# Output products of the first pair of blocks: 512 tokens streamed past 128 weight columns, and three attention steps moved

## The chip, the core and the metric

The kernel runs on one core of a Trainium2 chip. The metric is the device time of one execution in microseconds. Engines: TensorE (PE; its weight loads are listed as PEld), VectorE (DVE), ScalarE (ACT), GpSimd (POOL) and SyncE (SP), which only issues DMAs.

## What is computed

Attention over 4 batches, 8 heads of width 64, 512 local and 32 global tokens, then two dense layers over the 4 x 544 = 2176 rows of width 512:

```python
mask = np.abs(pos[:, None] - pos[None, :]) <= 32          # local queries: a window of 32, and all global keys
x = attention(q, k, v).reshape(2176, 512)                  # global queries see all keys
h = x @ moe_w_in                                           # 512 -> 2048
x = (np.maximum(h, 0) + alpha * np.minimum(h, 0)) @ moe_w_out
h = x @ moe2_w_in                                          # 512 -> 2048
out = (h * np.clip(h + 3.0, 0.0, 6.0) / 6.0) @ moe2_w_out
```

Everything is float32. The kernel splits every operand of the dense layers into a high part of reduced width (fp32r) and the low rest, and sums three products (high x high, high x low, low x high) in place of one.

## The kernel before

**Blocks.** The tokens come in five blocks: block 0, 1 and 2 are the 512 local tokens of batches 0, 1 and 2; block 3 is the first half of batch 3, block 4 its second half with the 128 global rows. Layer one runs block by block (the loop at the end of fused_kernel). In each step s an inner tile of 12 matmuls (h_tile, L590), its activation on ScalarE and VectorE (act, L600 to L609), and two steps later (LAG) an output group of 12 matmuls (y_tiles, L621) are issued. During block 0 the weights of layer one, which arrive as 64-bit numbers, are converted on ScalarE and VectorE (begin_float32, end_float32, L114 to L137); the same is done for layer two's weights during blocks 1 to 4 (second_weights), with the sums that Strassen's scheme wants; the results go to DRAM (wi, wo).

**Attention in between.** attention_steps(n), L639, runs n steps of the generator local_units; STEPS says how many there are in each step of a block. The units (batch, half, head pair) are taken in 16 pairs. For pairs 4 to 15 STARTS gives the step in which the scores are computed and WAITS how many steps later the value products follow: pair 5 has STARTS 4 and WAITS 4, pair 13 has STARTS 33 and WAITS 5. Step 1 of that list runs in step s = 4 of block 0, so step 8 is s = 11 there, step 32 is the last step with an inner tile of block 1 (s = 15), and step 33 the first of block 2. For pairs from 5 on the probabilities are turned: the step after the scores, VectorE transposes 32x32 blocks (turned, L285) and POOL sends the tile to DRAM (turn_out, L185); a step later POOL fetches it back in four pieces (turn_in, L191). The results of these pairs' value products (values, L299; the division L311; the block transpose L324) go the same way, except pair 7's, whose results, like pair 4's, are left as they are (L319) and turned by TensorE:

```python
steps[at][0].append((scores, *pairs[j]))
steps[at + wait][0].append((values, *pairs[j]))
```

**The change of blocks.** At s = end - 1 the loop makes sure that attention has come far enough (ready), calls x_transposed (L535), which issues TensorE's transposes of the results that are still unturned (L550, into a bank xt_ps), and then this step's y_tiles. At the last step x_split (L554) makes the next block's operands on ScalarE (L562) and VectorE (L563). All scores, value products, inner tiles and xt_ps take their turn in four PSUM banks (bank, tag "ps"); the outputs y have the other four.

**Layer two** (second_layer) works on two pairs of blocks in turn, twos: the first pair is blocks 1 and 2 (n = 0, 1024 tokens), the second block 0 with blocks 3 and 4 (n = 1, end is true). Each pair is a Strassen product of seven products with 512-token halves. First the inner products (product, L947): a weight part of 128 columns is loaded, 512 tokens stream past it. Then the output sums (summed, L1025): for each of the seven products and four groups k of inner rows, the operand is split into hi and lo (parts_of, L957: ScalarE L960, VectorE L961, three buffers), and for jp in 0 and 1 and each chunk c of 128 tokens three matmuls are issued:

```python
mm = nc.tensor.matmul(bank, lhsT=part[:, jp, 128 * c:128 * c + 128],
                      rhs=wo[:, jp, 256 * wl:256 * wl + 256], start=opens, ...
```

So 128 tokens are the loaded weight and 256 weight columns stream; the result has tokens on the partitions and is stored as it is (store, L1058: four DMAs of 128 rows and 256 columns per result, four results per pair). ScalarE copies or VectorE adds the sums out of PSUM (each, L1048; add, L877). Between the groups of the first pair, further work on the second pair's operands is issued (MORE, inputs, L774 to L793). In the second pair the 128 global rows ("the rest") have products of their own beside it (rest_in, L899; rest_out, L920). take (L854) keeps up to six weight tiles (512 KB each, ws) loading ahead through SyncE's queue, the one that the stores use too.

**Order.** Each engine works through its own queue in order. The program is written in the order above, and a planner then orders each engine's queue by its own estimate of times; instructions under here(...) keep their program order among themselves.

Of the kernel before, what the change touches and what calls it, by code (L numbers as in the profile page):

```python
# [19 lines left out]
S = SL + SG  # L20
# [16 lines left out]
STARTS = [0, 4, 8, 12, 16, 19, 22, 25, 29, 33, 36, 39]  # L37
GLOBAL = [[(x[0], int(x[1])) for x in part.split()] for part in "s0|t0|i0 s1|o0 t1|i1 s2|t2|o1 i2 s3|t3|o2 i3||o3".split("|")]
WAITS = [4, 4, 5, 4, 5, 5, 5, 5, 5, 5, 5, 5]
# [21 lines left out]
def fused_kernel(ctx, tc, qkE, vE, qgz, kN, vN, vgN, w1, w2, consts, out):  # L61
# [805 lines left out]
    def second_layer(bt):  # L867
# [45 lines left out]

        def rest_out(y, i, k, wo):

            kind, half = REST_OF[i]
            for jp in range(2):
                j = 2 * (2 * k + jp) + kind
                for wl, gl in ((0, 0), (1, 0), (0, 1)):
                    mm = nc.tensor.matmul(y[:, 256 * half:256 * half + 256],  # L920
                                     lhsT=gr[j // 4][:, gl, 128 * (j % 4):128 * (j % 4) + 128],
                                     rhs=wo[:, jp, 256 * wl:256 * wl + 256], start=i == k == jp == wl == gl == 0,
                                     stop=i in (2, 7) and k == NP // 2 - 1 and jp == gl == 1, skip_group_check=True)
                    if i == len(PRODUCTS) and k == jp == wl == gl == 0:
                        here(mm)
# [10 lines left out]
        for n, two in enumerate(twos):  # L936
# [43 lines left out]

            coming, split = operands(), []
# [43 lines left out]
            def summed(i, y, first=True):  # L1025
                for k in range(NP // 2):
# [3 lines left out]
                    for jp in range(2):  # L1030
                        for c in range(chunks):
                            bank = y[c // 2][:, 256 * (c % 2):256 * (c % 2) + 256]
                            for wl, part in ((0, hi), (1, hi), (0, lo)):
                                opens = first and k == jp == c % 2 == 0 and (wl, part is hi) == (0, True)
                                mm = nc.tensor.matmul(bank, lhsT=part[:, jp, 128 * c:128 * c + 128],  # L1035
                                                      rhs=wo[:, jp, 256 * wl:256 * wl + 256], start=opens,
                                                      stop=k == NP // 2 - 1 and jp == 1 and part is lo,
                                                      skip_group_check=True)
                                if opens and i == c == 0:
                                    here(mm)  # L1040
# [7 lines left out]
            def each(f, *lists):  # L1048
                for k, banks_ in enumerate(zip(*lists)):
                    f(slice(512 * k, min(512 * k + 512, 256 * chunks)), *banks_)  # L1050
# [4 lines left out]
            def cols(b, s_):  # L1055
                return b[:, 0:s_.stop - s_.start]

            def store(r, th, dm):  # L1058
                for c in range(chunks):
# [9 lines left out]
            each(lambda s_, b: nc.scalar.copy(m1[:, s_], cols(b, s_)), x_)  # L1069
            summed(1, y_)  # L1070
            m5 = result()
            each(lambda s_, b: nc.scalar.copy(m5[:, s_], cols(b, s_)), y_)
            summed(2, x_, False)
            c11 = result()
            each(lambda s_, b: nc.scalar.copy(c11[:, s_], cols(b, s_)), x_)
# [5 lines left out]
            each(lambda s_, b: add(m1[:, s_], m1[:, s_], cols(b, s_)), z_)  # L1081
            summed(4, y_, False)
            c12 = result()
            each(lambda s_, b: add(c12[:, s_], m1[:, s_], cols(b, s_)), y_)
# [4 lines left out]
            each(lambda s_, b: add(u3_[:, s_], m1[:, s_], cols(b, s_)), w_)  # L1089
# [5 lines left out]
            each(lambda s_, b: add(m1[:, s_], m1[:, s_], cols(b, s_)), w_)  # L1095
# [24 lines left out]
    for bi in range(len(blocks)):  # L1120
# [5 lines left out]
        for s in range(end + LAG):  # L1126
# [20 lines left out]
            if s == end - 1 and not last:  # L1147
# [3 lines left out]
                coming = x_transposed(blocks[bi + 1])  # L1151
            if s >= LAG:
                y_tiles(0, y, gs.pop(s - LAG), W1.wt, active(bi, s - LAG), bi == 0)
            done = [SPLIT[bi] * max(x - REST, 0) // (end + LAG - REST) for x in (s, s + 1)]
# [23 lines left out]
def _layout(q_l, k_l, v_l, q_g, k_g, v_g, moe_w_in, moe_w_out, moe_alpha, moe2_w_in, moe2_w_out):  # L1178
# [27 lines left out]
    def chunks(w_in, w_out):  # L1206
        a = w_in.reshape(NC, 128, NJ, 128).transpose(2, 1, 0, 3).reshape(NJ, 128, 512)
        return con(np.concatenate([a, w_out.reshape(NJ, 128, DM)], axis=2)).view(np.int64)

    r, c = np.arange(128)[:, None] % W, np.arange(128)[None, :]  # L1210
# [8 lines left out]
        "w1": chunks(moe_w_in, moe_w_out), "w2": chunks(moe2_w_in, moe2_w_out), "consts": consts,  # L1219
# [18 lines left out]
```

## Time and profile before

| | |
|---|---|
| median of 3 runs | 812.97 us (812.88 to 813.52) |
| the profiled execution | 818.06 us, span 816.3 us |
| mean granted TensorE clock | 0.994 of full speed |
| TensorE busy | 795.4 us (97%) |
| VectorE busy | 613.1 us (75%) |
| ScalarE busy | 409.8 us (50%) |
| DMA | 204.06 MB, 249 GB/s over the span to and from HBM |

The span runs from the first to the last instruction of the profiled execution. Its own time is 0.6% over the median of the runs. Stages in it: block 0 to about 144 us, block 1 to 244, block 2 to 345, blocks 3 and 4 to 471, the first pair of layer two to 632 (inner products to 549, output sums from there), the second pair to the end. Busy times of matmuls overlap, as they are pipelined; the time from one start to the next is read from the pieces of the chain.

### The profile page before, as it was taken

To read this page: it belongs to the slowest core of one execution; us is meant where nothing else is said; L and a number is where in the kernel's file an instruction comes from. 1 tells how busy PE (TensorE), PEld (TensorE's weight loads), DVE (VectorE), ACT (ScalarE), POOL (GpSimd) and SP (SyncE) were. 2 spreads that over 40 slices of the span, in tenths; PEclk is the share of its full clock that TensorE was granted. 3 is DMA by queue.
4 is the path that set the end of the run, shared out by engine and by line. 5 is a ranking of instruction groups with operands and counts; after the bars stand their busy time and mean duration, and the time that the engine had idled before them with its cause. 6 is when DMAs were issued, how large, how long until landed. Compare 5 with 4: busy or idle time off the path is not lost.

```text
span 816.3 us, 17563 instructions
## 1 busy us (share of the span) xinstructions
PE 795.4 (97%) x6812; PEld 696.2 (85%) x6812; DVE 613.1 (75%) x1307; ACT 409.8 (50%) x864; POOL 86.6 (11%) x141
## 2 busy tenths in 40 slices
PE   6999999999998999999999999999999999999998
PEld 4778777878886887788999988889999888899997
DVE  4889997678878887777899847778867576678443
ACT  5878886455546544544456434334543334333431
POOL 0332202122220322112000000000000000000000
PEclk9999999999999999999999999999999999999999
DMA  9978887489988889998995586676786666655663
GB/s 336 352 248 281 296 270 218 167 268 332 334 289 330 281 305 338 316 320 297 313 340 199 205 274 190 202 220 199 209 258 199 206 182 206 184 178 161 208 180 111
DMA packets 85507, 204.06 MB, mean 250 GB/s; under 512 B 8752, under 2 KB 31024, under 8 KB 85424
## 3 DMA queue, kind: packets, MB, share of 16 engines
q1 hardware_dynamic: 78112, 181.83, 67.2%
q0 software_dynamic: 7120, 20.98, 8.2%
q8 instruction: 54, 0.88, 0.5%
q14 instruction: 29, 0.24, 0.1%
q10 hardware_dynamic: 192, 0.13, 0.1%
HBM read 149.95 MB, written 52.95 MB: 249 GB/s over the span
## 4 chain that ended last, share of the span: by engine, by line
PE 79%; DMA 3%; DVE 1%; ACT 0%; issue 0%; SPq 0%; ACTq 0%
PE o_ps L1035 20%; PE k_ps L947 19%; PE y_ps L621 18%; PE h_ps L590 16%; DMA gk<-in_kN 2%; PE yr_ps L920 1%; PE hr_ps L899 1%; DMA xo<-turn 1%; PE o_ps L299 1%; PE s_ps L234 1%; PE gs_ps L440 1%; PE go_ps L477 0%; PE tr_ps L911 0%; PE xt_ps L550 0%; DVE p L260 0%
## 5 line engine op out<-in xcount | busy, mean ns | idle before, releaser
L590 PE MATMUL h_ps<-xt,wt 128*128 128x512 f32 (+2 forms) x1008 | 205.3, 353 | 2.4 <-DVE st L260 2.1
L621 PE MATMUL y_ps<-g,wt 128*128 128x512 f32 (+2 forms) x1008 | 206.4, 355 | 1.0 <-POOL wt L137 0.8
L590 PEld LDWEIGHTS h_ps<-xt,wt 128*128 128x128 f32 x1008 | 169.8, 191 | 25.8 <-issue 4.0
L621 PEld LDWEIGHTS y_ps<-g,wt 128*128 128x128 f32 x1008 | 168.8, 191 | 26.0 <-issue 2.4
L1035 PE MATMUL o_ps<-ws,gh 128*128 128x256 f32 x896 | 160.9, 283 | 0.1
L947 PE MATMUL k_ps<-bt,ws 128*128 128x512 f32 x672 | 157.2, 390 | 0.0
L947 PEld LDWEIGHTS k_ps<-bt,ws 128*128 128x128 f32 x672 | 124.6, 188 | 24.9
L1035 PEld LDWEIGHTS o_ps<-ws,gh 128*128 128x128 f32 x896 | 138.8, 192 | 0.6 <-issue 0.3
L1035 PE MATMUL o_ps<-ws,gl 128*128 128x256 f32 x448 | 124.2, 283 | 0.0
L961 DVE TENSOR_TENSOR gl<-far,gh 128x1024 fp32r<-128x1024 f32 x56 | 68.5, 1223 | 42.6 <-ACT gh L960 42.6
L960 ACT CAST gh<-far 128x1024 fp32r<-128x1024 f32 x56 | 58.7, 1049 | 74.7 <-PE o_ps L1035 70.9
L1035 PEld LDWEIGHTS o_ps<-ws,gl 128*128 128x128 f32 x448 | 84.9, 192 | 0.0
L881 ACT ACTIVATE t<-far,half_sb 128x512 f32<-128x512 f32 x48 | 34.8, 725 | 77.0 <-DVE far L877 77.0
L602 DVE SCALAR_TENSOR_TENSOR t<-t,c_sb,h_ps 128x512 f32<-128x512 f32 (+2 forms) x84 | 53.0, 641 | 17.9 <-ACT t L600 17.4
L600 ACT ACTIVATE t<-h_ps 128x512 f32<-128x512 f32 (+2 forms) x76 | 41.7, 550 | 47.0 <-PE h_ps L590 46.2
L608 ACT CAST g<-t 128x512 fp32r<-128x512 f32 (+2 forms) x76 | 43.7, 575 | 40.6 <-DVE t L602 37.7
L609 DVE TENSOR_TENSOR g<-t,g 128x512 fp32r<-128x512 f32 (+2 forms) x76 | 49.4, 653 | 10.9 <-ACT g L608 10.1
L265 ACT ACTIVATE p<-p,st 128x128 f32<-128x128 f32 x128 | 49.7, 392 | 10.0 <-DVE st L260 8.8
L114 ACT ACTIVATE raw<-raw,quarter_sb 128x512 uint32<-128x512 uint32 x64 | 49.2, 770 | 5.6 <-DMA raw<-in_w 5.6
L125 DVE SCALAR_TENSOR_TENSOR z<-z,raw 128x512 uint32<-128x512 uint32 x64 | 44.1, 695 | 5.0 <-ACT z L120 2.2
L127 DVE SCALAR_TENSOR_TENSOR z<-raw,z 128x512 uint32<-128x512 uint32 x64 | 44.7, 702 | 0.5
L882 DVE SCALAR_TENSOR_TENSOR far<-t,far 128x512 f32<-128x512 f32 x48 | 33.1, 689 | 11.8 <-ACT t L881 11.8
(110 smaller groups left out, 833.6 us busy)
## 6 DMA issues: line engine op xcount, KB each, us to landing
raw<-in_w SPq DMA_DIRECT2D x64, 512.0 KB, 7.1
ws<-wo SPq DMA_DIRECT2D x60, 512.0 KB, 3.9
ws<-wi SPq DMA_DIRECT2D x56, 512.0 KB, 4.7
v_t<-in_vE SPq DMA_DIRECT2D x32, 512.0 KB, 7.7
qk_t<-in_qkE SPq DMA_DIRECT2D x32, 368.0 KB, 5.7
wi<-raw SPq DMA_DIRECT2D x16, 512.0 KB, 5.4
wi<-parts SPq DMA_DIRECT2D x16, 512.0 KB, 6.3
wo<-raw SPq DMA_DIRECT2D x16, 512.0 KB, 5.8
```

What stands on the lines that cost most here:

```text
L114: here(nc.scalar.activation(low, low, AF.Relu, bias=quarter_sb, scale=0.9 * 2.0 ** -29))
L125: nc.vector.scalar_tensor_tensor(out=bits, in0=bits, scalar=3, in1=low, op0=ALU.logical_shift_left, op1=ALU.bitwise_or)
L127: nc.vector.scalar_tensor_tensor(out=bits, in0=high, scalar=0x80000000, in1=bits, op0=ALU.bitwise_and, op1=ALU.bitwise_or)
L265: nc.scalar.activation(to, to, AF.Exp, bias=st[:, 1, n:n + 1], scale=-1.0, accum_out=st[:, 2, n:n + 1])
L590: nc.tensor.matmul(ps[:, a:b], lhsT=wts[j][:, 0, wl, 128 * c:128 * c + 128], rhs=xt[c][:, xl, at:at + b - a], start=k == 0, stop=k == 3 * ...
L602: nc.vector.scalar_tensor_tensor(out=t[:, c:d], in0=t[:, c:d], scalar=c1_sb[:, j:j + 1], in1=ps[:, c:d], op0=ALU.mult, op1=ALU.add)
L609: nc.vector.tensor_tensor(out=g[:, 1, a:b], in0=t[:, a:b], in1=g[:, 0, a:b].bitcast(F32), op=ALU.subtract)
L621: nc.tensor.matmul(y[c][:, at:at + b - a], lhsT=wts[j][:, 1, wl, 128 * c:128 * c + 128], rhs=g[:, gl, a:b], start=first, stop=last, skip_g ...
L947: nc.tensor.matmul(bank, lhsT=wt[:, wl, 128 * c:128 * c + 128], rhs=bt[x][:, c, xl, 0:w], start=first and k == 0, stop=k == 5, skip_group_ ...
L960: nc.scalar.copy(hi, src)
L961: nc.vector.tensor_tensor(out=lo, in0=src, in1=hi.bitcast(F32), op=ALU.subtract)
L1035: mm = nc.tensor.matmul(bank, lhsT=part[:, jp, 128 * c:128 * c + 128], rhs=wo[:, jp, 256 * wl:256 * wl + 256], start=opens, stop=k == NP / ...
```

## The change

For the first pair (turned = not end) the sums load 128 columns of the streamed weight tile, c = 0 and 1, and stream 512 tokens. A result then has weight columns on the partitions and tokens along the row. The evictions write it in runs of 32 tokens so that after VectorE's transposes of 32x32 blocks each partition holds 64 result columns of 16 tokens; a store is four DMAs of 32 partitions, in pieces of 64 columns (256 bytes). To make the block transposes fit, the host lays out the columns of moe2_w_out in another order; where 256 weight columns stream as before (second pair and rest), in_order reads them in eight runs of 32. Pair 13's scores come one step earlier, at step 32, with its values at 38 as before; pair 5's values come one step later, at step 9. x_transposed is called after the step's y_tiles.

```diff
-STARTS = [0, 4, 8, 12, 16, 19, 22, 25, 29, 33, 36, 39]
+STARTS = [0, 4, 8, 12, 16, 19, 22, 25, 29, 32, 36, 39]
-WAITS = [4, 4, 5, 4, 5, 5, 5, 5, 5, 5, 5, 5]
+WAITS = [4, 5, 5, 4, 5, 5, 5, 5, 5, 6, 5, 5]
...
+        def in_order(w):
+            return w.rearrange("p (c b x) -> p b c x", c=2, b=4)
...
-                                     rhs=wo[:, jp, 256 * wl:256 * wl + 256], start=i == k == jp == wl == gl == 0,
+                                     rhs=in_order(wo[:, jp, 256 * wl:256 * wl + 256]), start=i == k == jp == wl == gl == 0,
...
+            turned = not end
...
-                    for jp in range(2):
+                    for jp in range(2) if turned else ():
+                        for c in range(2):
+                            k6 = 0
+                            for wl, part in ((0, hi), (1, hi), (0, lo)):
+                                at = 256 * wl + 128 * c
+                                opens = first and k == jp == k6 == 0
+                                mm = nc.tensor.matmul(y[c], lhsT=wo[:, jp, at:at + 128], rhs=part[:, jp, :], start=opens,
+                                                      stop=k == NP // 2 - 1 and jp == 1 and part is lo,
+                                                      skip_group_check=True)
...
+                    for jp in range(2) if not turned else ():
                         for c in range(chunks):
...
-                                                      rhs=wo[:, jp, 256 * wl:256 * wl + 256], start=opens,
+                                                      rhs=in_order(wo[:, jp, 256 * wl:256 * wl + 256]), start=opens,
...
             def each(f, *lists):
                 for k, banks_ in enumerate(zip(*lists)):
-                    f(slice(512 * k, min(512 * k + 512, 256 * chunks)), *banks_)
+                    f(lambda t: half_of(t, k), *[columns_of(b) for b in banks_])
+
+            def half_of(t, k):
+                return t.rearrange("p (a c x) -> p c a x", a=16, c=2)[:, k] if turned else t[:, 512 * k:512 * k + 512]
+
+            def columns_of(b):
+                return b.rearrange("p (a x) -> p a x", a=16) if turned else b
...
             def store(r, th, dm):
+                if turned:
+                    for at in range(0, 1024, 512):
+                        nc.vector.transpose(out=r[:, at:at + 512], in_=r[:, at:at + 512])
+                    to = rows[tiles[n][th][0][0], SG:S, 256 * dm:256 * dm + 256]
+                    for k in range(4):
+                        nc.sync.dma_start(out=to[:, 64 * k:64 * k + 64].rearrange("(a q) x -> q a x", q=32),
+                                          in_=r[32 * k:32 * k + 32].rearrange("q (a x) -> q a x", a=16))
+                    return
...
-            each(lambda s_, b: nc.scalar.copy(m1[:, s_], cols(b, s_)), x_)
+            each(lambda of, b: nc.scalar.copy(of(m1), b), x_)
...
-                coming = x_transposed(blocks[bi + 1])
             if s >= LAG:
                 y_tiles(0, y, gs.pop(s - LAG), W1.wt, active(bi, s - LAG), bi == 0)
+            if s == end - 1 and not last:
+                coming = x_transposed(blocks[bi + 1])
...
+    turned = moe2_w_out.reshape(-1, 2, 4, 2, 32).transpose(0, 1, 3, 2, 4).reshape(moe2_w_out.shape)
...
-        "w1": chunks(moe_w_in, moe_w_out), "w2": chunks(moe2_w_in, moe2_w_out), "consts": consts,
+        "w1": chunks(moe_w_in, moe_w_out), "w2": chunks(moe2_w_in, turned), "consts": consts,
```

The other evictions change in the same way as the one shown.

## Rows read from the trace of the kernel before

**Rows 1.** The page: busy time of the engines, and the chain by engine.

```profile
PE 795.4 (97%) x6812; PEld 696.2 (85%) x6812; DVE 613.1 (75%) x1307; ACT 409.8 (50%) x864; POOL 86.6 (11%) x141
...
PE 79%; DMA 3%; DVE 1%; ACT 0%; issue 0%; SPq 0%; ACTq 0%
```

**Rows 2.** Pieces of the chain, layer two: start us, us, what it was.

```profile
474.75 74.62 PE k_ps L947 x329
549.37 69.11 PE o_ps L1035 x576
...
620.32 11.51 PE o_ps L1035 x96
...
640.46 0.71 PE hr_ps L899 x6
```

**Rows 3.** Timeline, 62 to 86: start us, us, what [idle before <-releaser].

```profile
68.08 0.71 POOL L185 DMA_DIRECT2D turn<-p  x1 [4.08 <-DVE z L125]
...
76.37 2.20 POOL L191 DMA_DIRECT2D p<-turn  x4 [7.58 <-DMA turn<-p]
...
82.69 1.10 PE L299 MATMUL o_ps<-v_t,p 128*32 128x64 f32 x64 [1.40 <-DVE t L602]
```

**Rows 4.** Timeline, 119.5 to 146, at the change from block 0 to block 1.

```profile
134.48 0.41 ACT L562 CAST xt<-xo 128x256 fp32r<-128x256 f32 x1 [4.65 <-DMA xo<-turn]
...
136.22 0.66 PE L550 MATMUL xt_ps<-consts_sb,xo 128*128 128x128 f32 x4 [1.71 <-DVE t L602]
...
136.63 5.26 PE L621 MATMUL y_ps<-g,wt 128*128 128x512 f32 x22
...
143.76 0.42 DVE L563 TENSOR_TENSOR xt<-xt_ps,xt 128x256 fp32r<-128x256 f32 x1
...
144.25 1.98 PE L590 MATMUL h_ps<-xt,wt 128*128 128x512 f32 x8
```

**Rows 5.** Timeline, 215 to 262, at the change from block 1 to block 2.

```profile
241.71 0.71 ACT L562 CAST xt<-xo 128x256 fp32r<-128x256 f32 x2 [3.85 <-DMA xo<-turn]
...
245.10 1.12 PE L234 MATMUL s_ps<-qk_t 64*32 64x128 f32 x60
...
252.31 4.51 PE L590 MATMUL h_ps<-xt,wt 128*128 128x512 f32 x12 [2.10 <-DVE st L260]
```

**Rows 6.** Groups of VectorE by shape: count, busy us, mean ns; idle before.

```profile
L961 DVE TENSOR_TENSOR gl<-far,gh 128x1024 fp32r<-128x1024 f32 x56 | 68.5, 1223 | 42.6 <-ACT gh L960 42.6
...
L877 DVE TENSOR_TENSOR res<-res,o_ps 128x512 f32<-128x512 f32 x16 | 10.9, 686 | 5.6 <-PE o_ps L1035 5.4
...
L324 DVE STREAM_TRANSPOSE xo<-xo 128x512 f32<-128x512 f32 x10 | 7.0, 704 | 0.0
```

**Rows 7.** Stretches: us, busy by engine (instructions), granted clock, DMA share, GB/s.

```profile
252.30:256.80 4.50, 4.49 (x13) 3.56 (x14) 4.23 (x16) 2.83 (x11) 0.37 (x1) 0.62 0.98 359
...
549.40:632.00 82.60, 82.60 (x682) 82.22 (x681) 66.44 (x73) 37.93 (x47) 0.00 (x0) 1.00 0.72 218
560.90:595.40 34.50, 34.50 (x289) 34.50 (x289) 31.65 (x35) 18.26 (x23) 0.00 (x0) 1.00 0.69 201
```

**Rows 8.** DMA issues of SyncE, count, KB each, median us to landing.

```profile
ws<-wo SPq DMA_DIRECT2D x60, 512.0 KB, 3.9
...
out<-res SPq DMA_DIRECT2D x32, 128.0 KB, 3.1
```

**Rows 9.** Pieces of the chain at the changes of blocks.

```profile
130.28 4.13 DMA xo<-turn
...
236.64 4.97 DMA xo<-turn
...
259.66 2.72 PE h_ps L590 x12
```

**Rows 10.** Waits of TensorE, longest first: us in total, times, longest us.

```profile
PE xt_ps L550 <- DVE xo L319: 3.9, 2, 2.6
...
PE gs_ps L440 <- DMA gk<-in_kN: 0.5, 1, 0.5
```

More of the change, by code (lines that the diff above doesn't have):

```diff
@@ L1029, in summed @@
                     wo = take("sum", n, i, k)
-                    for jp in range(2):
+                    for jp in range(2) if turned else ():
[7 more added lines that the diff above has]
+                                                      skip_group_check=True)
+                                k6 += 1
+                                if opens and i == c == 0:
+                                    here(mm)
+                    for jp in range(2) if not turned else ():
                         for c in range(chunks):
@@ L1049, in each @@
                 for k, banks_ in enumerate(zip(*lists)):
-                    f(slice(512 * k, min(512 * k + 512, 256 * chunks)), *banks_)
+                    f(lambda t: half_of(t, k), *[columns_of(b) for b in banks_])
[3 more added lines that the diff above has]
+                return b.rearrange("p (a x) -> p a x", a=16) if turned else b
             def result():
                 return pair_temp("res").rearrange("p h c -> p (h c)")
-            def cols(b, s_):
-                return b[:, 0:s_.stop - s_.start]
             def store(r, th, dm):
+                if turned:
[6 more added lines that the diff above has]
+                    return
                 for c in range(chunks):
@@ L1068, in second_layer @@
             m1 = result()
-            each(lambda s_, b: nc.scalar.copy(m1[:, s_], cols(b, s_)), x_)
+            each(lambda of, b: nc.scalar.copy(of(m1), b), x_)
             summed(1, y_)
             m5 = result()
-            each(lambda s_, b: nc.scalar.copy(m5[:, s_], cols(b, s_)), y_)
+            each(lambda of, b: nc.scalar.copy(of(m5), b), y_)
             summed(2, x_, False)
             c11 = result()
-            each(lambda s_, b: nc.scalar.copy(c11[:, s_], cols(b, s_)), x_)
+            each(lambda of, b: nc.scalar.copy(of(c11), b), x_)
             store(c11, 0, 0)
@@ L1080, in second_layer @@
             summed(3, z_)
-            each(lambda s_, b: add(m1[:, s_], m1[:, s_], cols(b, s_)), z_)
+            each(lambda of, b: add(of(m1), of(m1), b), z_)
             summed(4, y_, False)
             c12 = result()
-            each(lambda s_, b: add(c12[:, s_], m1[:, s_], cols(b, s_)), y_)
+            each(lambda of, b: add(of(c12), of(m1), b), y_)
             store(c12, 0, 1)
@@ L1088, in second_layer @@
             u3_ = result()
-            each(lambda s_, b: add(u3_[:, s_], m1[:, s_], cols(b, s_)), w_)
+            each(lambda of, b: add(of(u3_), of(m1), b), w_)
             for at in range(0, 256 * chunks, 512):
@@ L1094, in second_layer @@
             summed(6, w_, False)
-            each(lambda s_, b: add(m1[:, s_], m1[:, s_], cols(b, s_)), w_)
+            each(lambda of, b: add(of(m1), of(m1), b), w_)
             store(m1, 1, 0)
```

## The prediction

> **What bounds the kernel now.** I read the page's busy times and its chain first. TensorE is busy for 97% of the span and holds 79% of the chain that ended last; VectorE is busy for 75% [rows 1]. So time is saved only by shortening TensorE's own stream or by closing one of its few gaps. The page's busy figure for TensorE hides the pace of its stream, since pipelined matmuls overlap in it; the pieces of the chain show the pace. In the output sums of the first pair 576 matmuls of 256 columns take 69.11 us, 120.0 ns each, and 96 more take 11.51 us, 119.9 ns; in the inner products 329 matmuls of 512 columns take 74.62 us, 226.8 ns each [rows 2]. Twice as many columns therefore cost 1.89 times as much, and 2 x 120.0 - 226.8 = 13.2 ns is what one matmul costs beyond its columns. Next, the gaps: the timeline shows TensorE idle 1.40 us before the value products at 82.69 [rows 3], 1.71 us before the transposes at 136.22 [rows 4], and 2.10 us before the block at 252.31 [rows 5]. The three shifts of attention work and the later call of x_transposed lie at these three places.
>
> **The streamed products.** For the first pair the change issues 7 products x 4 groups x 2 x 2 x 3 = 336 matmuls of 512 columns where 672 of 256 columns stood (7 x 4 x 2 x 4 x 3: in place of four token chunks, two halves of the result's columns). The columns streamed stay the same. The form with 128 weight columns of the streamed weight and 512 moving columns already runs in the inner products, so its pace is measured: 336 x (2 x 120.0 - 226.8) = **-4.4 us**, all of it on TensorE's path, where these sums run without a break [rows 2]. The inner products load weights as often per column as these will, so I give this term no range of its own.
>
> **What VectorE and the queue get for it.** Each of the first pair's four results is turned by two 128x512 block transposes: 8 x 0.704 = 5.6 us on VectorE [rows 6]. The evictions (16 adds of 0.686 us in both pairs) keep their number and size and now write in runs of 32 words; ScalarE's copies too. I cost that at nothing, as they hide behind the next product. The cover is thin, though. In 549.4 to 632 VectorE is busy 66.4 of 82.6 us; with 5.6 more and 4.4 less it would be 72.0 of 78.2. In the densest part, 560.9 to 595.4, it is busy 31.65 of 34.5 us [rows 7]; those twelve groups will take 12 x 12 x 0.2268 = 32.7 us on TensorE, and the first result's transposes (1.4 us) come into it: 33.05 us of work. TensorE catches up on it by 0.4 us there, and the splits are made two groups ahead. I take **+0.5 us**, bounds 0 and +2.0 (the first result's transposes, and half as much again at the step into the second pair). If this cover goes, the next group's low part (1.223 us each [rows 6]) is what comes late.
>
> The 16 stores of the first pair stay 16 SyncE issues of 128 KB, now of 256-byte pieces where they had 1 KB pieces. They land in 3.1 us today, and the weight loads queued behind them in 3.9 us [rows 8]; six weight tiles are held ahead, some 6 x 2.7 = 16 us of products, so a store four times as slow would still not be seen. I cost it at 0; the other end, a late weight tile, has no row below 256-byte pieces, and I bound it by one landing more, 3.9 us. The Trainium skill (DMA: Bandwidth & Descriptors, Specifications) asks for at least 512 B per transfer for full rate and so speaks against these stores. By that rule the stores slow down, and the sum stays as it is for the reason just given; no run here yet shows a 256-byte store.
>
> **The moving operand in pieces.** In the second pair, 7 x 4 x 2 x 4 x 3 = 672 matmuls, and the 96 of the rest, now read their 256 moving columns as 8 runs of 32. The nearest row is the rest's inner product, whose 256 columns come as two runs of 128: 6 in 0.71 us, 118 ns, no dearer than one run [rows 2]. I take 0, from that row. The other end is that every one of the 7 further runs costs what starting a matmul costs, 13.2 ns: 768 x 7 x 13.2 = 71 us. A gain is excluded, since no column is saved.
>
> **Pair 5's values one step later.** Its probabilities come back by DMAs that POOL issues at 76.37 (four, 2.20 us in all), because the outward transfer issued at 68.08 had first to land; TensorE stands before the products at 82.69 for 1.40 us [rows 3]. The profile names VectorE's t as the last to come; with the DMAs only 4 to 6 us old either may be the releaser, and a step later both are past. The step later has an inner tile and an output group in front of these products, over 5 us of work, so the wait goes: **-1.4 us**, bounds 0 and -1.4. What moves along: the division and the block transpose on VectorE, one outward DMA and four inward ones on POOL, now behind pair 6's outward transfer, and pair 6's value loads on SyncE, which wait for these products' buffers. Pair 5's results are wanted only for the next block's operands, some 50 us later [rows 4], pair 6's values four steps of over 5 us later, so I cost them at 0.
>
> **x_transposed after y_tiles.** ScalarE sits 4.65 us on the DMA of pair 6's results, which lands near 134.4, and only then evicts the inner tile whose bank the transposes need; TensorE waits 1.71 us with 22 ready output matmuls behind them [rows 4]. With the output group first, 2.7 us of work lies before the transposes and the gap closes, even if TensorE arrives 1.4 us earlier. Next late are the splits of the next block: the last VectorE split starts at 143.76 and the block's first inner product at 144.25 [rows 4], so with TensorE 3.1 us ahead about 1.0 us of the gain would be waited for there. I take **-0.7 us**, bounds 0 and -1.7.
>
> **Pair 13's scores one step earlier.** Today its last 60 score products run at 245.10, after the block change; VectorE works off its backlog before the maxima, and TensorE waits 2.10 us at 252.31 for the bank they release [rows 5]. A step earlier the scores come before the block's last three output groups, 3 x 2.72 = 8.2 us sooner, and ScalarE stands idle 3.85 us after them, until 241.71, for a DMA that takes 4.97 us from 236.64 [rows 5, 9]. Even if the softmax is queued behind that, it has 7 us more than now. The products themselves (1.1 us) change places and cost the same. One load pair on SyncE and the block transposes, with one outward DMA on POOL, also come a step earlier; they are queued behind pair 12's, whose values keep their place. Gap: **-2.1 us**, bounds 0 and -2.1. Right behind this gap the granted clock falls to 0.62 over 252.3 to 256.8, part of the time at 1.2 instead of 2.4 GHz [rows 7], and twelve matmuls take 4.51 us where 2.72 is usual [rows 5, 9]. Without the gap this goes too: **-1.8 us**, bounds 0 and -1.8.
>
> **The sum.** -4.4 + 0.5 - 1.4 - 0.7 - 2.1 - 1.8 = -9.9. Moving work between in-order queues seldom leaves all others alone: TensorE's listed waits reach from 0.5 to 2.6 us [rows 10], and I add one of about 1.0 us. That makes -8.9. The profiled execution took 818.06 us for a span of 816.3, 0.6% over the median of 812.97; differences of a few us carry over unscaled: 812.97 - 8.9 = **804.1 us**, own range 801.6 (all upper gains, no loss) to 807.0.
>
> **Rivals.** (1) The shifted steps only move their waits, because these hang on DMAs and VectorE rather than on the order; the pieces 4.13 and 4.97 us long of the chain speak for it [rows 9], the banks named above against it. Then -4.4 + 0.5 + 1.0 = -2.9: 810.1 us. Chance 0.20. (2) VectorE becomes the bound of the first pair's sums: all 2.0 us, and 1.4 more for the second half of the transposes at the step into the second pair; -9.9 + 2.9 + 1.0 = -6.0, 807.0 us. The 31.65 of 34.5 speaks for it, the rest of the stage against: 66.44 - 31.65 = 34.8 us in 48.1. Chance 0.09. (3) Slower: the moving operand in 8 runs breaks TensorE's stream in the 768 matmuls of the second pair. It decides from (8.9 + 1.6) / 768 = 13.7 ns per matmul; at two matmul starts each (26.4 ns) it costs 20.3 us and gives 824.4 us. For it: no row has such short runs; against it: the two-run row at no price. Chance 0.09. The Trainium skill (Advanced Engine Details and Errata, Memory Cachelines) says both that non-contiguous patterns in PSUM slow matmuls markedly and that SBUF accesses run at full rate while neighbours share a 16-byte line. Its first sentence, carried over to this operand, would give rival 3, its second the forecast; no run here shows either yet. (4) The planner orders the queues so that neither part is seen, or a new wait eats both: 812.5 us, chance 0.05.
>
> **Chances.** Forecast 0.57, rivals 0.20, 0.09, 0.09, 0.05. Within 0.2% (1.6 us), about what a measurement of this kernel can tell from no change, lies rival 4; slower is rival 3; the rest is faster: 0.86. The range takes in the forecast, rival 2 and rival 1 to 811.0, and 801.0 below.
>
> **What would show it.** Right: first-pair sums as 336 matmuls at 227 ns, about 76 us; second-pair ones at 120 ns; no gap of over 0.5 us before the value products near 83, the transposes near 136 and the block near 250; a clock of 1.00 there; eight more 128x512 transposes on VectorE with TensorE not waiting behind them. Wrong: second-pair matmuls above 125 ns, gaps of TensorE before first-pair groups that end with the low part, or the same gaps some steps later.

## The result and the profile after

The changed kernel takes **806.84 us** (median of 4 runs, 805.73 to 806.96) against 813.25 us (4 runs, 812.88 to 818.12) for the kernel before beside it: ratio **0.9903**, 95% interval 0.9874 to 0.9931, or -7.9 us (-10.2 to -5.6). The ratio weighs all runs, the one of 818.12 too (the means differ by 7.8 us); the two medians differ by 6.4 us. Forecast were -8.9 us and 804.1 us; the time lies within the range, 0.2 us below the upper end of the forecast's own range (801.6 to 807.0). The profiled execution took 806.96 us.

The page after: span, and busy time of the engines [rows 1].

```profile
span 805.2 us, 16896 instructions
...
PE 791.0 (98%) x6476; PEld 677.6 (84%) x6476; DVE 617.8 (77%) x1315; ACT 409.4 (51%) x864; POOL 86.9 (11%) x141
```

Pieces of the chain after, layer two: start us, us, what it was [rows 2].

```profile
469.03 74.62 PE k_ps L950 x329
543.64 65.28 PE o_ps L1040 x288
...
724.15 14.27 PE o_ps L1051 x120
```

The first pair's sums take 65.28 / 288 = 226.7 ns for each matmul, as forecast, and TensorE waits for nothing in them. The 120 matmuls without a break in the second pair take 118.9 ns each. Before, they took 120.0; the same piece there:

```profile
734.40 14.40 PE o_ps L1035 x120
```

The timeline after, at the value products of pair 5 [rows 3] and the change from block 0 to block 1 [rows 4], then at the change from block 1 to block 2 [rows 5]; in brackets the idle time before, and what ended it.

```profile
88.57 1.10 PE L299 MATMUL o_ps<-v_t,p 128*32 128x64 f32 x64
...
132.66 1.10 PE L299 MATMUL o_ps<-v_t,p 128*32 128x64 f32 x64 [0.26 <-DMA p<-turn]
...
136.32 0.60 PE L550 MATMUL xt_ps<-consts_sb,xo 128*128 128x128 f32 x4
...
241.68 5.79 PE L590 MATMUL h_ps<-xt,wt 128*128 128x512 f32 x24
247.40 1.10 PE L299 MATMUL o_ps<-v_t,p 128*32 128x64 f32 x64
248.43 3.01 PE L590 MATMUL h_ps<-xt,wt 128*128 128x512 f32 x12
251.28 2.88 PE L621 MATMUL y_ps<-g,wt 128*128 128x512 f32 x12
```

None of the three gaps of 1.40, 1.71 and 2.10 us is left. New ones are smaller: 0.26 us at 132.66, before pair 7's values, 0.38 us at 305.91, before other value products, and one before the weight load of the global scores, which waits for their keys (timeline of PEld after, near 319):

```profile
319.33 0.15 PEld L440 LDWEIGHTS gs_ps<-gk,gq 64*32 64x32 f32 x8 [1.10 <-DMA gk<-in_kN]
```

VectorE's new group by shape, and the DMA groups [rows 8], after:

```profile
L1080 DVE STREAM_TRANSPOSE res<-res 128x512 f32<-128x512 f32 x8 | 5.2, 689 | 0.0
```

```profile
ws<-wo SPq DMA_DIRECT2D x60, 512.0 KB, 4.0
...
out<-res SPq DMA_DIRECT2D x32, 128.0 KB, 3.3
```

The group out<-res holds the stores of both pairs, and only the first pair's are in 256-byte pieces. Taken by their line, the first pair's 16 stores alone, after (L1083) and then before (L1062, window 540 to 640):

```profile
DMA to landing us min/median/max: 2.6/3.7/5.1
```

```profile
DMA to landing us min/median/max: 1.7/3.9/4.3
```

So the median of the stores in small pieces is no later there. The second pair's stores, in 1 KB pieces in both kernels, land in 2.1 us after and 2.2 before.

To split the 7.9 us, I divide each profiled execution where the 329 inner matmuls of layer two start: ahead of that lies layer one with attention (where the shifts work), behind it layer two (where the streaming works).

| kernel | layer one, us | layer two, us | ratio to before |
|---|---|---|---|
| before (the one forecast from) | 474.75 | 341.55 | |
| before_again | 470.99 | 341.51 | |
| stream_only | 471.58 | 336.12 | 0.9935 |
| steps_only | 466.98 | 341.22 | 0.9953 |
| after | 469.03 | 336.17 | 0.9903 |
| pair13_only | 470.23 | 341.57 | 0.9986 |
| transposes_tripled | 466.83 | 337.17 | 0.9903 |
| both_streamed | 467.70 | 334.80 | 0.9862 |
| runs_all | 471.63 | 340.17 | 0.9976 |
| runs_of_4 | 471.74 | 352.56 | 1.0129 |
| runs_of_1 | 469.12 | 329.68 | 0.9828 |
| words_other | 471.42 | 447.08 | 1.1334 |
| words_steps | 468.50 | 329.50 | 0.9825 |
| words_inner | 470.61 | 324.99 | 0.9820 |

Layer two repeats within 0.4 us between executions with the same matmuls; layer one scatters by 2 us and more (469.12 to 474.75 among the kernels without the shifts).

### The profile page after: what moved, and what is told of

The parts are those of the page before. It is cut to its first block, busy times and chain, and to the rows that moved or that the text cites. A ratio compares the mean times of both kernels' runs of the same rounds, so it can differ in the third digit from the quotient of the medians.

```text
span 805.2 us, 16896 instructions
## 1 busy us (share of the span) xinstructions
PE 791.0 (98%) x6476; PEld 677.6 (84%) x6476; DVE 617.8 (77%) x1315; ACT 409.4 (51%) x864; POOL 86.9 (11%) x141
## 4 chain that ended last, share of the span: by engine, by line
PE 78%; DMA 8%; DVE 7%; issue 4%; ACT 3%; SPq 0%; POOL 0%; DVEq 0%; ACTq 0%; POOLq 0%
PE k_ps L950 19%; PE y_ps L621 17%; PE h_ps L590 16%; PE o_ps L1051 10%; PE o_ps L1040 9%; DMA gk<-in_kN 2%; DMA raw<-in_w 1%; PE yr_ps L923 1%; PE hr_ps L899 1%; ACT p L265 1%; DMA p<-turn 1%; DVE z L125 1%; PE o_ps L299 1%; PE s_ps L234 1%; DMA turn<-xo 1%
## 5 line engine op out<-in xcount | busy, mean ns | idle before, releaser
L621 PEld LDWEIGHTS y_ps<-g,wt 128*128 128x128 f32 x1008 | 167.0, 189 | 26.0 <-issue 2.2
L1051 PE MATMUL o_ps<-ws,gh 128*128 128x256 f32 x448 | 80.5, 282 | 0.1
L1051 PEld LDWEIGHTS o_ps<-ws,gh 128*128 128x128 f32 x448 | 68.8, 189 | 0.4 <-issue 0.3
L1040 PE MATMUL o_ps<-gh,ws 128*128 128x512 f32 x224 | 64.9, 389 | 0.0
L1051 PE MATMUL o_ps<-ws,gl 128*128 128x256 f32 x224 | 62.7, 282 | 0.0
L265 ACT ACTIVATE p<-p,st 128x128 f32<-128x128 f32 x128 | 49.6, 389 | 11.3 <-DVE st L260 10.3
L1040 PEld LDWEIGHTS o_ps<-gh,ws 128*128 128x128 f32 x224 | 42.1, 188 | 8.8
```

Source lines behind the costliest of these rows:

```text
L265: nc.scalar.activation(to, to, AF.Exp, bias=st[:, 1, n:n + 1], scale=-1.0, accum_out=st[:, 2, n:n + 1])
L621: nc.tensor.matmul(y[c][:, at:at + b - a], lhsT=wts[j][:, 1, wl, 128 * c:128 * c + 128], rhs=g[:, gl, a:b], start=first, stop=last, skip_g ...
L1040: mm = nc.tensor.matmul(y[c], lhsT=wo[:, jp, at:at + 128], rhs=part[:, jp, :], start=opens, stop=k == NP // 2 - 1 and jp == 1 and part is ...
```

## The experiments

**The kernel before once more**, with no edit, to see which of its gaps return.

> The kernel before, unchanged, looked at once more. Theory 1 (the forecast's): the three drops of the granted clock and the gap of TensorE near 367 seen in the first profile belong to the kernel, so they come again and the profiled execution takes about 818 us. Theory 2: they belong to that one execution, which lay 5 us over the median; then this one takes about 813 us, with the gaps of 1.4, 1.7 and 2.1 us near 83, 136 and 252 still there, but the clock at 1.00 around 252 to 257, so that closing the last gap is worth 2.1 us and not 3.9.

Measured: 814.3 us, in the middle of the kernel's other runs beside it (median 814.97). TensorE's waits, longest first (us in total, times, longest):

```profile
...
PE h_ps L590 <- DVE st L260: 2.2, 1, 2.2
PE xt_ps L550 <- DVE t L602: 2.1, 1, 2.1
PE o_ps L299 <- DMA p<-turn: 1.7, 1, 1.7
```

All three gaps return, and this time pair 5's wait names the fetch p<-turn, the releaser that the forecast had held possible beside VectorE's t. The fall of the clock behind the 2.2 us does not return: theory 2. There is one elsewhere, behind the gap before the transposes (timeline and windows):

```profile
135.95 1.11 PE L550 MATMUL xt_ps<-consts_sb,xo 128*128 128x128 f32 x4 [2.11 <-DVE t L602]
...
135.00:140.00 5.00, 4.05 (x13) 3.40 (x14) 4.93 (x26) 4.19 (x19) 0.00 (x0) 0.66 0.75 249
```

From these transposes to the next ones it takes 7.0 us there (to 142.96) and 5.5 in the execution forecast from, where the clock stayed at 1.00 behind 1.71 us. Later runs kept this order of attention too, so the spot near 252 could be read seven times. Here are the twelve matmuls behind its gap in runs_of_4 and in runs_of_1 (timeline), each followed by the stretch around them (windows; the granted clock is the third number from the end):

```profile
252.42 4.58 PE L590 MATMUL h_ps<-xt,wt 128*128 128x512 f32 x12 [1.94 <-DVE st L260]
...
252.00:257.00 5.00, 4.58 (x13) 3.69 (x14) 4.74 (x20) 3.24 (x13) 0.47 (x1) 0.66 0.99 359
```

```profile
250.89 2.97 PE L590 MATMUL h_ps<-xt,wt 128*128 128x512 f32 x12 [2.05 <-DVE st L260]
...
252.00:257.00 5.00, 5.00 (x24) 4.14 (x23) 4.73 (x15) 2.31 (x6) 0.56 (x1) 1.00 1.03 392
```

With almost the same gap the clock falls in one and stays at 1.00 in the other. (In one of the seven, words_other, the gap was 0.86 us; in the others 1.87 to 2.18.) It fell in two of the seven (the execution forecast from, and runs_of_4) and in none of the seven without the gap. When it falls it costs 1.5 to 1.6 us (4.51 and 4.58 against 2.97 to 3.01).

**The streamed products alone**: the changed kernel with the attention steps put back.

```diff
-STARTS = [0, 4, 8, 12, 16, 19, 22, 25, 29, 32, 36, 39]
-WAITS = [4, 5, 5, 4, 5, 5, 5, 5, 5, 6, 5, 5]
+STARTS = [0, 4, 8, 12, 16, 19, 22, 25, 29, 33, 36, 39]
+WAITS = [4, 4, 5, 4, 5, 5, 5, 5, 5, 5, 5, 5]
...
+                coming = x_transposed(blocks[bi + 1])
             if s >= LAG:
                 y_tiles(0, y, gs.pop(s - LAG), W1.wt, active(bi, s - LAG), bi == 0)
-            if s == end - 1 and not last:
-                coming = x_transposed(blocks[bi + 1])
```

> Only the first pair's sums streamed past the weight columns, with the host's column order, the block transposes and the stores that belong to it; STARTS, WAITS and the place of x_transposed as before. Theory 1 (forecast's sum): -4.4 + 0.5 = -3.9 us, ratio 0.995, with TensorE waiting now and then in the first pair's sums. Theory 2 (from the changed kernel's trace): -4.4 with no wait, and another -0.8 us as the 768 matmuls whose moving columns come in eight runs take 118.9 ns instead of 120: -5.2 us, ratio 0.9936.

Measured: 808.74 us, ratio 0.9935 (0.9916 to 0.9955), -5.3 us. Pieces of its chain:

```profile
471.58 74.61 PE k_ps L950 x329
546.20 65.28 PE o_ps L1040 x288
...
726.70 14.28 PE o_ps L1051 x120
```

From the inner matmuls to the 120 of the second pair it takes 255.12 us; the kernel before takes 734.40 - 474.75 = 259.65. That is -4.53, the term of the streaming with nothing lost to VectorE. From there to the end of the span it takes 81.00 in place of 81.90, -0.9, from matmuls that read shorter runs. Theory 2 holds.

**The three shifts alone**: the kernel before with the new STARTS and WAITS and x_transposed behind y_tiles (the lines above, the other way round).

> Only the three shifts: STARTS and WAITS of pairs 5 and 13, and x_transposed after y_tiles; the sums as before. Theory 1 (forecast's sum): -1.4 - 0.7 - 2.1 - 1.8 + 1.0 = -5.0 us, ratio 0.994. Theory 2: without the clock's 1.8 us and with new waits on the DMAs of the global keys near 319 (1.2 us) and of x near 400 (0.5 us): -1.4 - 1.2 - 2.1 + 1.7 = -3.0 us, ratio 0.996. If rival 1 of the forecast were true, within 1 us of the kernel before.

Measured: 810.16 us, ratio 0.9953 (0.9933 to 0.9974), -3.8 us. Waits of TensorE:

```profile
...
PE o_ps L299 <- DMA p<-turn: 1.4, 1, 1.4
...
PE xt_ps L550 <- DVE t L602: 0.7, 1, 0.7
```

The wait for p<-turn of 1.4 us now stands at 131.98, before pair 7's values. That pair 5's gain carries TensorE into the next fetch is a reading; for it speaks that this wait is in four of the six executions with all three shifts (0.26 us in the changed kernel, 1.23 in transposes_tripled, 0.52 in words_inner) and in none of the eight with pair 5's old place. So part of the shifts' gain moves on, as rival 1 had it, and most stays.

**Pair 13's scores alone**, on the kernel before.

```diff
-STARTS = [0, 4, 8, 12, 16, 19, 22, 25, 29, 33, 36, 39]
+STARTS = [0, 4, 8, 12, 16, 19, 22, 25, 29, 32, 36, 39]
-WAITS = [4, 4, 5, 4, 5, 5, 5, 5, 5, 5, 5, 5]
+WAITS = [4, 4, 5, 4, 5, 5, 5, 5, 5, 6, 5, 5]
```

> The kernel before, with pair 13's scores one step earlier and nothing else of the change. The forecast: the gap of 2.1 us before the third block's first inner tile and the 1.8 us of halved clock behind it both go, -3.9 us, ratio 0.9952. Theory 2 (the fall of the clock belongs to single executions, not to the gap): -2.1 us, ratio 0.9974, with TensorE going from the second block's last tile to the third's without a wait; the gaps of 1.4 and 1.7 us near 83 and 133 us stay. Rival (the wait only moves): a wait of about the same length elsewhere in the two steps, ratio 1.000.

Measured: 813.37 us, ratio 0.9986 (0.9970 to 1.0003), -1.1 us. The timeline shows the gap gone, and two waits further on (the second line is of PEld):

```profile
249.00 3.01 PE L590 MATMUL h_ps<-xt,wt 128*128 128x512 f32 x12
...
319.46 0.15 PEld L440 LDWEIGHTS gs_ps<-gk,gq 64*32 64x32 f32 x8 [1.08 <-DMA gk<-in_kN]
...
345.20 1.10 PE L477 MATMUL go_ps<-gv,gp 128*32 128x64 f32 x64 [0.69 <-ACT t L600]
```

The gain is made at the place forecast and partly given back 70 to 95 us later, at the global keys and ScalarE. Theory 2's 0.9974 lies in the interval, the forecast's 0.9952 does not. The rival's 1.000 lies in it too, so by time alone a gain of this one shift is not shown; that its gap closes is. Pair 5 and x_transposed were not tried alone, nor an earlier load of the global keys.

**All output matmuls in 8 runs of 32** (the kernel before with the new order of the output weights and in_order; against stream_only it is one line).

```diff
-            turned = not end
+            turned = False
```

> The kernel before with only the host's column order changed and every output product of layer two, of both pairs and of the rest, reading its 256 moving columns in eight runs of 32: 1344 + 96 matmuls. Theory 1 (forecast's price): no difference, 120.0 ns per matmul. Theory 2: 118.9 ns per matmul, -1.6 us, ratio 0.998. Rival 3 of the forecast: more than 13.7 ns longer per matmul, at least +20 us.

Measured: 812.79 us, ratio 0.9976 (0.9957 to 0.9995). Chain:

```profile
546.25 68.53 PE o_ps L1051 x576
...
730.55 14.27 PE o_ps L1051 x120
```

119.0 and 118.9 ns: shorter runs are a little quicker than one run of 256, in both pairs. That asked for other lengths.

**Runs of 4 words, then of 1** (as runs_all, with in_order and the host's order changed together; here for 1):

```diff
-            return w.rearrange("p (c b x) -> p b c x", c=2, b=4)
+            return w.rearrange("p (c b x) -> p b c x", c=2, b=128)
...
-    turned = moe2_w_out.reshape(-1, 2, 4, 2, 32).transpose(0, 1, 3, 2, 4).reshape(moe2_w_out.shape)
+    turned = moe2_w_out.reshape(-1, 2, 128, 2, 1).transpose(0, 1, 3, 2, 4).reshape(moe2_w_out.shape)
```

> The kernel before, but for the order of the output weights: all 1440 output matmuls of layer two read their 256 moving columns as 64 runs of 4 words (16 bytes), alternating between the two halves of the tile, where eight runs of 32 took 118.9 ns. Theory 1 (the length of a run costs nothing down to 16 bytes, as the Trainium skill has it in Advanced Engine Details and Errata, Memory Cachelines): 118.9 ns as with eight runs, ratio 0.998. Theory 2 (every run costs something, rival 3 of the prediction in a weaker form): above 120.0 ns and growing with the runs, at 1 ns for each of 56 further runs 175 ns and 81 us in all, ratio 1.10. Theory 3 (each change of half saves something, since 8 runs saved 1.1 ns): below 118 ns.

> The kernel before, but for the order of the output weights: all 1440 output matmuls of layer two read their 256 moving columns one word at a time, alternating between the two halves of the tile. Theory 1 (neighbours have to share 16 bytes): twice the 107 ns that 256 columns take beyond the 13.2, 226 ns or more for each, some 1440 x 107 = 154 us, ratio 1.19 or more. Theory 2 (the moving operand's layout inside a partition does not matter at all): 118.9 ns, ratio 0.998.

Measured: 825.72 us, ratio 1.0129 (1.0088 to 1.0170), for runs of 4; **800.93 us, ratio 0.9828** (0.9797 to 0.9859), for single words. The same piece of each chain, runs of 4 first:

```profile
546.36 72.97 PE o_ps L1051 x576
```

```profile
543.73 64.32 PE o_ps L1051 x576
```

126.7 and 111.7 ns. None of the theories had both. Single words that alternate between places 128 words apart save 8.3 ns for a matmul; 13.2 ns is what one costs beyond its columns.

**A fixed step of two words** (first pair), **and pairs of words** (second pair), on the order of runs_of_1; the evictions put the columns right.

```diff
+            def read(w):
+                if not end:
+                    return w.rearrange("p (b c) -> p c b", c=2)
+                return w.rearrange("p (c b x) -> p b c x", c=2, x=2)
...
-                                                      rhs=in_order(wo[:, jp, 256 * wl:256 * wl + 256]), start=opens,
+                                                      rhs=read(wo[:, jp, 256 * wl:256 * wl + 256]), start=opens,
```

> The kernel before, with the output weights in the order of the word-by-word run; the first pair's 672 matmuls read the columns with a fixed step of two words (0, 2, 4, ..., then 1, 3, ...), the second pair's 672 in pairs of words that alternate between the halves, and the copies out of PSUM put the columns right. Theory 1 (any word that is not the last one's neighbour helps): 111.7 ns with the step of two. Theory 2 (only the alternation between places 128 words apart helps): 120.0 ns or more with the step of two. Pairs of words: between the 126.7 ns of runs of 4 and the 111.7 ns of single words if the run's length decides, 119 ns in the middle.

Measured: 921.48 us, ratio 1.1334. Chain, step of two, then pairs:

```profile
546.03 132.48 PE o_ps L1057 x576
...
809.33 20.40 PE o_ps L1057 x120
```

230.0 ns with the step of two, 170.0 with pairs. Theory 1 is out, and theory 2's 120.0 ns or more holds: a word that isn't the last one's neighbour does not help by itself. Alternating between places 128 words apart helped with single words and with runs of 32, and cost time with runs of 4 and with pairs, where 119 ns had been expected. And the length of the run does not order the times: 120.0 (one run), 118.9 (32), 126.7 (4), 170.0 (2), 111.7 (1).

**VectorE's cover**: each result of the first pair turned three times over (three block transposes make one).

```diff
-                    for at in range(0, 1024, 512):
+                    for at in 3 * (0, 512):
```

> The changed kernel, with each result of the first pair turned three times over (a block transpose done three times is one transpose): 16 more transposes of 128x512, 11.3 us of VectorE beside the first pair's sums and the step into the second pair. Theory 1 (VectorE's cover there is ample, which is why the +0.5 of the forecast was not seen): first inner product of layer two to the second pair's output sums stays at 255.1 us, ratio 0.990 as the changed kernel. Theory 2 (the cover is as thin as the forecast has it, 72.0 of 78.2 us): 83.3 us of VectorE's work no longer fit, TensorE waits before groups that end with the low part, some 2 to 5 us in all, and the stretch grows to 257 to 260 us, ratio 0.993 to 0.996.

Measured: 806.99 us, ratio 0.9903 (0.9869 to 0.9937). A window of the first pair's sums (us, then busy of PE, PEld, DVE), and TensorE's only wait in 541 to 640 (a weight load has 0.9 more there):

```profile
552.00:587.00 35.00, 35.00 (x156) 29.00 (x155) 34.79 (x38) 18.12 (x23) 0.00 (x0) 1.00 0.67 197
...
PE k_ps L950 <- ACT ab L1002: 0.4, 1, 0.4
```

VectorE is busy for 34.79 of 35.0 us and TensorE still for all of them; the stretch that was 255.12 us grows to 256.16, and the 1.0 us is lost at the step into the second pair. So 11.3 us more cost 1.0: nearer to theory 1, and the 5.6 us of the change cost nothing that shows.

**The second pair streamed too.**

```diff
-            turned = not end
+            turned = True
```

> The changed kernel, with the second pair's sums streamed in the same way (turned for both pairs; the 96 matmuls of the rest keep their eight runs of 32). Theory 1 (streaming is worth 2 x 120.0 - 226.8 ns for each pair of matmuls, wherever it is used, since VectorE's transposes hide): 336 matmuls of about 227 ns in the second pair too, 4.4 us less there, of which 0.75 us goes again because 672 matmuls of 118.9 ns, already quicker than 120.0, are replaced: against the kernel before -7.9 - 3.7 = -11.6 us, ratio 0.986. Theory 2 (the second pair has less cover: the rest's products bring VectorE more work, and the transposes and finely cut stores of the last results lie at the end of the span): the 3.7 us are eaten, ratio 0.990, like the changed kernel.

Measured: 804.00 us, ratio 0.9862 (0.9835 to 0.9890), as theory 1 has it; but that is partly luck: layer two shows only 334.80 against 336.17, -1.4 us in place of -3.7, and the rest is layer one's scatter. The end of the span tells why. Timeline, both_streamed and then the changed kernel:

```profile
795.00 1.30 DVE L1080 STREAM_TRANSPOSE res<-res 128x512 f32<-128x512 f32 x2
796.33 2.22 SPq L1083 DMA_DIRECT2D out<-res  x4
797.13 0.37 ACT L934 COPY rz<-yr_ps 128x256 f32<-128x256 f32 x1 [8.83 <-PE yr_ps L923]
...
798.66 1.51 SPq L937 DMA_DIRECT2D out<-rz  x2
```

```profile
798.77 1.80 SPq L1089 DMA_DIRECT2D out<-res  x4
801.63 0.37 ACT L934 COPY rz<-yr_ps 128x256 f32<-128x256 f32 x1 [9.18 <-PE yr_ps L923]
802.02 0.80 SPq L937 DMA_DIRECT2D out<-rz  x2
```

The transposes make the last results 1.3 us late, and their four stores hold SyncE's queue when the rest's rows are ready at 797.5: these go out at 798.66, and the span ends 5.37 us after the copy began in place of 3.57. That is 1.8 us of the 2.3 us missing. Theory 2 is right about the end of the span.

**Both gains without streaming**: the order of runs_of_1 with the three shifts.

> The three shifted steps, with no product streamed: instead all 1440 output matmuls of layer two read their 256 moving columns word by word, alternating between the halves of the tile, which took 111.7 ns each against 120.0 and made 13.4 us. If the two gains add up: -13.4 - 3.8 = -17.2 us against the kernel before, ratio 0.979, and 9 us under the changed kernel, whose streamed matmuls take 226.7 ns for what two of these do in 223.4. If the gain of the word order was one of that run: ratio 0.995, as the shifted steps alone.

Measured: **800.12 us, ratio 0.9825** (0.9799 to 0.9850), -14.3 us: faster than the changed kernel, whose interval ends at 0.9874. Layer two takes 329.50 us against 336.17. It lies no lower than runs_of_1 without the shifts (0.9828), so no further gain of the shifts shows here; each interval is some 5 us wide, and whether they add up stays open.

**The inner products word by word too**: their operands are stored in that order, and read so.

```diff
+    def by_words(t):
+        return t.rearrange("p (h c b) -> p h b c", c=2, b=128)
...
-            x = bt[name][:, c, :, 0:n]
-            nc.scalar.copy(x[:, 0, :], src)
+            x, src = bt[name][:, c, :, 0:n], src.rearrange("p (h b c) -> p h b c", c=2, b=128)
+            nc.scalar.copy(by_words(x[:, 0, :]), src)
...
-                        nc.tensor.matmul(bank, lhsT=wt[:, wl, 128 * c:128 * c + 128], rhs=bt[x][:, c, xl, 0:w],
+                        nc.tensor.matmul(bank, lhsT=wt[:, wl, 128 * c:128 * c + 128], rhs=by_words(bt[x][:, c, xl, 0:w]),
```

> As the shifted steps with the output weights read word by word, and layer two's inputs stored so that its 672 inner matmuls of 512 columns read their moving operand word by word too, alternating between places 128 words apart. Theory 1 (the 8.3 ns are saved once for a matmul, out of the 13.2 ns that one costs beyond its columns): 218.5 ns in place of 226.8, 5.6 us less, ratio 0.972. Theory 2 (they are saved by column, 8.3 ns for each 256): 210 ns, 11.2 us less, ratio 0.965. Theory 3 (they hang on the tile that the weights of the stream lie in, or on the 256 columns): 226.8 ns, ratio 0.979.

Measured: 798.69 us, ratio 0.9820 (0.9788 to 0.9852). Chain of words_inner, then VectorE's low parts of the operands by shape (count, busy us, mean ns; idle before) in it and in words_steps:

```profile
470.61 71.21 PE k_ps L954 x329
...
L793 DVE TENSOR_TENSOR bt<-xt,bt 128x512 fp32r<-128x512 f32 x16 | 18.2, 1135 | 2.5 <-ACT bt L792 2.3
```

```profile
L790 DVE TENSOR_TENSOR bt<-xt,bt 128x512 fp32r<-128x512 f32 x16 | 11.0, 686 | 1.4 <-ACT bt L789 1.4
```

216.4 ns in place of 226.8: about 10 ns saved once for a matmul, nearest to theory 1. Layer two gains 4.5 us of the 672 x 10.4 = 7.0 us, as VectorE's and ScalarE's late parts now stop TensorE in it; layer one is 2.1 us longer than in words_steps, in which its scatter and the slower writing of single words by turns into places 128 words apart (1135 ns a time in place of 686) cannot be told apart.

## Why the prediction was right, and where its terms were off

That the sum was right is luck in part: two errors of opposite sign nearly cancelled. **Layer two** gave 341.5 - 336.15 = -5.4 us where the forecast had -4.4 + 0.5 = -3.9. **Layer one** gave about -3.3: five executions with the shifts and plain inner operands (after, steps_only, transposes_tripled, both_streamed, words_steps) reach the inner products at 467.8 us on average, six without any (before_again, stream_only and the four with the weights reordered) at 471.1. With the two executions that this omits (the one forecast from, and words_inner) the means are 471.6 and 468.3, the same difference. The forecast had -1.4 - 0.7 - 2.1 - 1.8 + 1.0 = -5.0. The measured time also fits rival 2's 807.0 us; what excludes that rival is that TensorE waits for nothing in the streamed sums.

Layer one's account can be followed by the starts of the same matmuls, on average over the six executions with the three shifts and the seven without any. At the output group behind pair 13's place near 252 the shifted ones are 4.8 us ahead (250.6 against 255.4), at the global value products near 345 4.2 us (342.9 against 347.1), at the inner products of layer two 3.3 us. So about 1.5 us is handed back behind the places of the shifts.

- *Streamed products, -4.4*: right. 226.7 ns each, -4.53 in the stretch.
- *VectorE, "I take +0.5 us"*: mis-sized; 0, the lower bound, was measured. The step counted VectorE's busy share as if it had to fit within each window. The tripled transposes show that even 34.79 of 35.0 us leaves TensorE unharmed there. Rival 2 falls with it.
- *Stores of 256 bytes, 0*: right in the first pair, where their median is 3.7 us until they land, against 3.9 for the 1 KB pieces before. (The forecast's 3.1 us is the median of both pairs' stores, not of the first pair's.) That the cover matters shows where there is none: at the end of the span, turned results and their stores cost 1.8 us. The Trainium skill (DMA: Bandwidth & Descriptors, Specifications) asks for at least 512 bytes for full rate. The traces agree only in the second pair, where both_streamed's 256-byte stores land in 2.9 us and the changed kernel's 1 KB pieces in 2.1; in the first pair no loss shows.
- *Moving operand in pieces, "A gain is excluded, since no column is saved"*: **this step failed.** 768 matmuls became 1.1 ns shorter, 0.85 us. The step took the time of a matmul to be its columns and a fixed start; with the same columns it hangs on the order in which they are read, too. Rival 3 was wrong for runs of 32, but its mechanism exists: pairs of words cost 50.0 ns more than one run, far over the 13.7 ns from which it decides.
- *Pair 5, -1.4*: right in size for the gap, 1.42 us on average in the eight executions with the old place (0.89 to 1.74) and gone in the six with the new one. Its releaser is not one thing: the profiles name VectorE in five of the eight and the fetch p<-turn in three. Pair 7's wait for the same kind of fetch gives back 0.6 us on average of the six (0 to 1.42).
- *x_transposed, -0.7*: the gap of 1.71 us is gone, with 0.70 us left of it in steps_only. In eight executions with the old order the gap is anything from 0 to 2.11 us, 1.0 on average; what the move is worth by itself was not tried.
- *Pair 13, gap -2.1*: the gap went; by itself it measures -1.1 us (+0.2 to -2.4), and part of the gain is given back further on.
- *Clock, "Without the gap this goes too: -1.8 us"*: **this step failed.** It took a fall that one execution showed for a property of the kernel. The clock fell behind that gap in 2 of 7 executions at 1.5 to 1.6 us, so the term is worth some 0.4 us on average. (The step's 1.8 also set 4.51 us from a timeline against 2.72 from a chain; undisturbed, the twelve show 2.97 to 3.01 in a timeline.) With it goes "differences of a few us carry over unscaled": the profiled 818.06 us held falls near 252 and 370 that before_again, at 814.3 us, does not have there; its own lies at 136.
- *New wait, +1.0*: near in size. 0.26, 0.38 and 1.10 us make 1.7 in the profiled execution of the changed kernel; its place was left open by the forecast. The longest, about 1 us for the global keys, is no fixed price: it is in the changed kernel, pair13_only, words_steps, words_inner and also in words_other without any shift, and not in steps_only, transposes_tripled and both_streamed.

Rival 1, that the shifts only move their waits, is excluded as a whole by steps_only (0.9933 to 0.9974) and right in part, as pairs 7 and 13 show.

## What to carry to other kernels

Before a term is taken from a profile, look whether the median run pays it: here a fall of the clock, in a profiled execution 5 us over the median, belonged mostly to that execution. The same holds for a gap: the one before the transposes was 0 to 2.1 us long in eight executions of one order. Close gaps of an engine in order and look at what stands next: a gain early in a stage is partly handed to the next fixed release, here a fetch of probabilities or a load of keys. And where a matmul's pace differs from its columns by a constant, try the order in which the moving operand is read before restructuring: reading single words alternately gave 14 us with a few changed lines, streaming with its transposes 5. Each pattern has to be measured, as pairs of words cost 50 ns for each matmul.

## What the runs showed that was not expected

The time of a matmul of 256 moving columns depends on the reading pattern of that operand, and not in one direction: 120.0 ns in one run, 118.9 in runs of 32, 126.7 in runs of 4, 170.0 in pairs, 111.7 in single words (all alternating between places 128 words apart), and 230.0 with a step of two words. The Trainium skill (Advanced Engine Details and Errata, Memory Cachelines) says that SBUF reads keep full rate while subsequent ones share a 16-byte line and pay when each goes to another. The runs do not agree for this operand: with a step of two, two words share a line and the time nearly doubles; alternating single words never share one with the word before and are the fastest. Why was not settled.

Also, the granted clock fell behind the same gap of about 2 us in two executions and not in four, so a single profile cannot say whether a gap costs its clock.
